# First group of a fused attention + MoE kernel: the weight round moves from the start of a step to the end of the step before, and its last call follows the others

## Chip, cores and metric

The kernel runs on one core of one Trainium2 chip. The metric is device time in microseconds (us) of one launch. Engines are named as in the profile: PE (TensorE matmuls), PEld (TensorE weight loads), DVE (VectorE), ACT (ScalarE), POOL (GpSimd), SP (SyncE; here it only issues DMAs).

## What is computed

Local attention with block summaries, then a feed-forward layer with the Mish activation, all in fp32. Cut from the reference:

```python
B, H, S, D = 4, 8, 768, 64;  block, window = 32, 16
k_sum = k.reshape(B, H, nb, block, D).max(axis=3)       # key maxima per block of 32
v_sum = v.reshape(B, H, nb, block, D).mean(axis=3)      # value means per block of 32
scores = concat(where(|i - j| < 16, scale * q @ k^T, -1e9), scale * q @ k_sum^T + log(32))
x = softmax(scores) @ concat(v, v_sum)                  # -> (3072 tokens, 512)
h = x @ w_in                                            # 512 -> 2048
out = (h * tanh(softplus(h))) @ w_out                   # 2048 -> 512
```

The weights come as 64-bit words (fp64 bits) that the kernel turns into fp32 itself.

## The kernel before

**Units and groups.** Attention works in units (c, hp): 256 queries c and a pair of heads hp; 48 units. Feed-forward works in 6 groups g of 512 tokens, 16 steps fc each (128 of the 2048 hidden columns). Units 0 to 7 are done ahead of the loop; the loop `for i in range(len(steps) + 2)` then does in step i the feed-forward step (g, fc) = divmod(i, 16) and, at the steps in the table `at` (0, 4, 8, 12 in the first group), the scores of two more units, whose values are formed four steps later.

**Order.** The program is under a manual schedule: each engine runs its instructions in the order in which the code emits them, waiting in place for what is not ready. So the order of the calls in a step is the order on every engine and on SP's queue.

**fp32 by splitting.** Each fp32 matmul is three passes: high part times high, high times low, low times high. `ff_in` (L406) gives `ph`, 12 matmuls; `ff_act` (L413) gives `a` (Mish, ACT); `ff_split` gives the high part `ah` (L422, ACT in the first group, DVE later) and the low part `al` (L424, DVE); `ff_out` (L434) adds `w_out`'s part into `po`, 12 matmuls, two steps later.

**Weights, first group only.** 16 pieces, each two steps of `w_in` (w0_k) or `w_out` (w1_k), taken in the order w0_0, w0_2, w1_0, w0_4, w1_2, w0_6, w1_4, w0_8, w1_6, w0_10, w1_8, w0_12, w1_10, w0_14, w1_12, w1_14. A piece passes five calls:

- `load_weight`: two DMAs from SP (L124) into one of two staging buffers. SP waits until `begin_weight` has read the piece that lay there;
- `begin_weight`: `f` on ACT (L136) and `x` on DVE (L138, L140);
- `join_weight`: `f` clamped, shifted and joined with `x` on DVE (L148, L150);
- `upper_weight`: the high part `w_hi` on ACT (L158), which needs the joined `f`;
- `lower_weight`: the low part `w_lo` on DVE (L165), which needs `w_hi`.

I call the first four of them with `lower_weight` a *round*. Each call takes the next piece in its own queue, so a round works on up to five different pieces.

**Attention work that shares the engines.** For a batch (b) and head pair: `ks` is loaded (L201) and its maxima `km` taken on DVE (L244); `vsum` is loaded (L205) into the same buffer (there is one), and its sums `vq` (L264, L265) go out by a DMA `vm` (L266). So the chain is ks, km, vsum, vq, then the next ks. POOL copies `km` into the unit's keys `qk` (L275), and the scores `sc` (L311, PE) of a unit need that copy: first 16 matmuls for the first unit of a pair, then 16 for the second. DVE takes the row maxima `pr`, `nm` (L333), ACT the exponentials (L337), DVE the reciprocals `rs` (L347, L348), POOL the product `pr` (L351). PE transposes (`pt_ps`, L359), ACT copies to `pt` (L361), PE forms `x_ps` (L391), ACT and DVE split it into `xh` (L393) and `xl` (L394).

**A step of the first group before the change**, in the order of the calls: upper, join, begin, load; `rs` and POOL's product (steps 1, 5, 9, 13); `ff_in`, `ff_act`, `ah`; `x_ps` and `xh` (steps 4, 8, 12); scores, maxima and exponentials (steps 0, 4, 8, 12); `lower_weight`; `xl`; `al`; then `vq` or `km` and the DMAs of the attention; `ff_out` of two steps ago; transposes and the `pt` copies (steps 3, 7, 11, 14).

Of the kernel before, what the change touches and what calls it, by code (L numbers as in the profile page):

```python
# [52 lines left out]
def _as_f32(bits):  # L53
    import struct
    return struct.unpack("<f", struct.pack("<I", bits))[0]
# [3 lines left out]
def fused_kernel(ctx: ExitStack, tc: tile.TileContext, q0, qk, kt, v0, vw, vs, w_in, w_out, out):  # L59
# [46 lines left out]
    def home(j, part, dtype, name):  # L106

        if j == NW:
            t = stage.tile([P, WB, WP], I64, tag="stage", name=name).bitcast(dtype)
            return t.rearrange("p k f -> p (k f)")[:, :WB * WP]  # L110
        pool = const if j < EARLY else late[0]
        return pool.tile([P, WB * WP], dtype, tag=f"w{part}_{j}", name=name, bufs=1)
# [6 lines left out]
    def load_weight():  # L119
        if weights:  # L120
            w, fc = weights.pop(0)
            t = stage.tile([P, WB, WP], I64, tag="stage", name=f"w{w}_{fc}")
            for k in range(WB):
                nc.sync.dma_start(t[:, k, :], (w_in, w_out)[w][fc + k])  # L124
            loaded.append((w, fc, t))

    def begin_weight():
        if loaded:
            w, fc, t = loaded.pop(0)
            j = order[w, fc]  # L130
            flat = t.rearrange("p k f -> p (k f)")
            high = flat.bitcast(U32).rearrange("p (f two) -> p f two", two=2)[:, :, 1]
            quarter = flat.bitcast(U16).rearrange("p (f four) -> p f four", four=4)
            x = home(j, 0, U32, f"x{w}_{fc}")
            f = home(j + 1, 1, F32, f"f{w}_{fc}")
            nc.scalar.activation(f, high.bitcast(F32), AF.Copy, scale=2.0 ** -OFFSET)  # L136
            half = x.bitcast(U16).rearrange("p (f two) -> p f two", two=2)
            nc.vector.tensor_scalar(out=half[:, :, 0], in0=quarter[:, :, 1], scalar1=13, scalar2=None,  # L138
                                    op0=ALU.logical_shift_right)
            nc.vector.tensor_scalar(out=half[:, :, 1], in0=quarter[:, :, 3], scalar1=SIGN, scalar2=None,  # L140
                                    op0=ALU.bitwise_and)
            begun.append((w, fc, f, x))

    def join_weight():
        if begun:
            w, fc, f, x = begun.pop(0)
            u = f.bitcast(U32)
            nc.vector.tensor_scalar(out=f, in0=f, scalar1=-_as_f32(F32_MAX), scalar2=_as_f32(F32_MAX),  # L148
                                    op0=ALU.max, op1=ALU.min)
            nc.vector.scalar_tensor_tensor(out=u, in0=u, scalar=3, in1=x,  # L150
                                           op0=ALU.logical_shift_left, op1=ALU.bitwise_or)
            joined.append((w, fc, f))

    def upper_weight():
        if joined:
            w, fc, f = joined.pop(0)
            split[w, fc, 0] = home(order[w, fc], 0, F32R, f"w{w}_{fc}_hi")
            nc.scalar.copy(split[w, fc, 0], f)  # L158
            raised.append((w, fc, f))

    def lower_weight():
        if raised:
            w, fc, f = raised.pop(0)
            split[w, fc, 1] = home(order[w, fc], 1, F32R, f"w{w}_{fc}_lo")
            nc.vector.tensor_sub(split[w, fc, 1], f, split[w, fc, 0].bitcast(F32))  # L165
# [117 lines left out]
    def att_summarize_values(c, hp):  # L283
        b, th = divmod(c, CPB)
        if th == 0:
            value_summary(b, hp)
# [56 lines left out]
    def att_normalize(group):  # L343
        n = len(group) * NQ
        u = units[group[0]]
        rs = small.tile([P, 2 * NQ], F32, tag="rs", name=f"rs{group[0][0]}_{group[0][1]}")[:, :n]
        nc.vector.tensor_scalar_add(rs, u["sm"][:, :n], 1e-9)  # L347
        nc.vector.reciprocal(rs, rs)  # L348
        if u.get("squares"):
            nc.gpsimd.memset(u["wide"][:, :, KA:], 0.0)  # L350
        nc.gpsimd.tensor_mul(u["pr"], u["pr"], rs.unsqueeze(2).broadcast_to([P, n, KA]))  # L351
# [11 lines left out]
    def att_transpose_blocks(group, half):  # L363

        u = units[group[0]]
        if half == 0:
            u["tr"] = att.tile([P, 2 * NQ, P], F32, tag="pt", name=f"pt{group[0][0]}_{group[0][1]}", bufs=1)
            for k, unit in enumerate(group):
                units[unit]["pt"] = u["tr"][:KA, k * NQ:(k + 1) * NQ]
        for a in range(2 * half, 2 * half + 2):  # L370
            for b in range(P // SQ):
                nc.vector.transpose(u["tr"][b * SQ:(b + 1) * SQ, :, a * SQ:(a + 1) * SQ],  # L372
                                    u["wide"][a * SQ:(a + 1) * SQ, :, b * SQ:(b + 1) * SQ])
# [26 lines left out]
    def ff_in(g, fc):  # L400
        xh, xl = xs[g]
        ph = ps_w.tile([P, TG], F32, tag="w", name=f"ph{g}_{fc}")
        wh, wl = (weight(0, part, fc) for part in range(2))
        for cc in range(NCC):
            for n, (w, x) in enumerate(((wh, xh), (wh, xl), (wl, xh))):
                nc.tensor.matmul(ph, w[:, cc * P:(cc + 1) * P], x[:, cc, :],  # L406
                                 start=(cc == 0 and n == 0), stop=(cc == NCC - 1 and n == 2))
        st[g, fc] = ph

    def ff_act(g, fc):  # L410

        a = ff.tile([P, TG], F32, tag="t", name=f"a{g}_{fc}", bufs=2)
        nc.scalar.activation(a, st[g, fc], AF.Mish)  # L413
        st[g, fc] = a

    def ff_split(g, fc):

        a = st[g, fc]
        ah = ff.tile([P, TG], F32R, tag="ah", name=f"ah{g}_{fc}")
        al = ff.tile([P, TG], F32R, tag="al", name=f"al{g}_{fc}")  # L420

        (nc.scalar.copy if g == 0 else nc.vector.tensor_copy)(ah, a)  # L422
        st[g, fc] = ah, al
        return lambda: nc.vector.tensor_sub(al, a, ah.bitcast(F32))  # L424
# [86 lines left out]
    values = dict(zip(turns[1:] + [turns[-1] + 4], (at[i] for i in turns)))  # L511
    turned = {i + (3 if i < NFC - 4 else 2): group for i, group in at.items() if i < NFC - 1}
    following = dict(zip(turns, (at[i] for i in turns[1:])))
    for i in range(len(steps) + 2):
        upper_weight()
        join_weight()
        begin_weight()
        load_weight()
        if i - 1 in at and i < NFC:
            att_normalize(at[i - 1])  # L520
        if i < len(steps):
            ff_in(*steps[i])
            ff_act(*steps[i])
            if i < NFC:
                split_rest = ff_split(*steps[i])
        group = values.get(i)
        lower = att_values(group) if group else None
        if lower and i >= NFC:
            lower()
        if i in at:  # L530
            att_scores(at[i], i >= NFC - 1)
        lower_weight()
        if i < NFC:
            if lower:
                lower()
            split_rest()
        if i - 1 in at and i >= NFC:
            att_normalize(at[i - 1])
        if i - 3 in at and i - 3 >= NFC - 1:
            att_transpose_blocks(at[i - 3], 1)  # L540
        if NFC <= i < len(steps):
            ff_split(*steps[i])()
        if i - 2 in at and i - 2 >= NFC - 1:
            att_transpose_blocks(at[i - 2], 0)
        if i - 3 in following:
            n, m = following[i - 3]
            att_summarize_values(*m)
            after = todo.index(m) + 1
            if after < len(todo) and todo[after][0] % CPB == 0:
                load_key_source(todo[after][0] // CPB, todo[after][1])  # L550
        if i in following:
            n, m = following[i]
            att_summarize_keys(*n)
            for unit in (n, m):
                att_load_keys(*unit)
        if i - 1 in following:
            n, m = following[i - 1]
            att_summarize_values(*n)
            if m[0] % CPB == 0:
                load_key_source(m[0] // CPB, m[1])  # L560
        if i - 2 in following:
            n, m = following[i - 2]
            att_summarize_keys(*m)
            for unit in (n, m):
                att_block_keys(*unit)
        if group:
            for unit in at.get(i, ()):
                att_load_values(*unit)
        if i >= 2:
            ff_out(*steps[i - 2])  # L570
        if i in turned:
            att_transpose(turned[i])
# [44 lines left out]
```

## Time and profile before

| | us |
|---|---|
| median of 3 runs | 633.23 (633.0 to 634.34) |
| the profiled execution | 633.05 |
| its span, first to last instruction | 630.9 |
| PE busy | 604.1 (96%) |
| DVE busy | 385.8 (61%) |
| ACT busy | 258.8 (41%) |
| POOL busy | 78.7 (12%) |

A row of the timeline reads: start in us from the span's start, length in us (of the whole row, where it stands for several instructions, x2), engine, line of the kernel, operation, names out<-in, shapes, and in square brackets the idle time of the engine just before it with what ended it. In the view by windows each row is a stretch: its length, then busy us and number of instructions of PE, PEld, DVE, ACT, POOL, then the TensorE clock granted (1.00 is full), the DMA engines' busy share and GB/s. Consecutive instructions of an engine overlap a little, so what an instruction costs its engine is the distance from its start to the start of the next.

The first matmul of the first group's feed-forward starts at 45.0 us, and its steps 0 to 12 take until about 128 us.

### The profile page before, as it was taken

To read this page: it belongs to the slowest core of one execution; us is meant where nothing else is said; L and a number is where in the kernel's file an instruction comes from. 1 tells how busy PE (TensorE), PEld (TensorE's weight loads), DVE (VectorE), ACT (ScalarE), POOL (GpSimd) and SP (SyncE) were. 2 spreads that over 40 slices of the span, in tenths; PEclk is the share of its full clock that TensorE was granted. 3 is DMA by queue.
4 is the path that set the end of the run, shared out by engine and by line. 5 is a ranking of instruction groups with operands and counts; after the bars stand their busy time and mean duration, and the time that the engine had idled before them with its cause. 6 is when DMAs were issued, how large, how long until landed. Compare 5 with 4: busy or idle time off the path is not lost.

```text
span 630.9 us, 10795 instructions
## 1 busy us (share of the span) xinstructions
PE 604.1 (96%) x4096; PEld 495.1 (78%) x4096; DVE 385.8 (61%) x1032; ACT 258.8 (41%) x630; POOL 78.7 (12%) x119
## 2 busy tenths in 40 slices
PE   5859999799999999999999999999999999999997
PEld 4747887588888888788888888888888888888886
DVE  4678999982855667855656758756647636222221
ACT  3759867675334244245144244153253251111111
POOL 4441020221011011011011010110110110000000
PEclk9979999999999999999999999999999999999999
DMA  8957587733223043533033241532232010100001
GB/s 273 319 191 249 215 271 238 220 115 97 92 72 122 2 146 122 169 98 97 0 98 96 92 147 55 169 99 88 75 97 82 16 33 0 68 0 1 0 1 66
DMA packets 31779, 69.26 MB, mean 110 GB/s; under 512 B 4720, under 2 KB 11120, under 8 KB 31728
## 3 DMA queue, kind: packets, MB, share of 16 engines
q1 hardware_dynamic: 31728, 68.58, 34.2%
q8 instruction: 32, 0.52, 0.4%
q14 instruction: 19, 0.16, 0.1%
HBM read 60.16 MB, written 6.29 MB: 105 GB/s over the span
## 4 chain that ended last, share of the span: by engine, by line
PE 78%; DMA 7%; DVE 7%; ACT 3%; issue 2%; SPq 1%; POOL 0%; DVEq 0%; ACTq 0%; POOLq 0%
PE po L434 37%; PE ph L406 35%; DMA vw<-vw 3%; PE x_ps L391 3%; PE sc L311 3%; DMA w<-w_out 2%; DMA w<-w_in 1%; DVE w_lo L165 1%; DVE al L424 1%; DVE x L138 1%; ACT f L136 1%; ACT pr L337 1%; DVE x L140 1%; DVE f L148 1%; DMA ks<-kt 1%
## 5 line engine op out<-in xcount | busy, mean ns | idle before, releaser
L413 ACT ACTIVATE a<-ph 128x512 f32<-128x512 f32 x96 | 57.2, 596 | 284.1 <-PE ph L406 230.6
L434 PE MATMUL po<-w_hi,ah 128*128 128x512 f32 x384 | 152.0, 396 | 0.7 <-ACT ah L422 0.5
L434 PE MATMUL po<-w_hi,al 128*128 128x512 f32 x384 | 149.9, 390 | 1.4 <-DVE al L424 1.4
L406 PE MATMUL ph<-xh,w_hi 128*128 128x512 f32 x384 | 150.7, 393 | 0.0
L406 PE MATMUL ph<-xl,w_hi 128*128 128x512 f32 x384 | 150.2, 391 | 0.0
L406 PE MATMUL ph<-xh,w_lo 128*128 128x512 f32 x384 | 150.0, 391 | 0.0
L434 PE MATMUL po<-w_lo,ah 128*128 128x512 f32 x384 | 149.6, 390 | 0.0
L422 DVE CAST ah<-a 128x512 fp32r<-128x512 f32 x80 | 34.6, 433 | 144.1 <-ACT a L413 143.6
L372 DVE STREAM_TRANSPOSE pt<-pr 32x256 f32<-32x256 f32 x256 | 111.5, 436 | 3.6
L434 PEld LDWEIGHTS po<-w_hi,ah 128*128 128x128 f32 x384 | 72.1, 188 | 19.0 <-issue 3.0
L434 PEld LDWEIGHTS po<-w_hi,al 128*128 128x128 f32 x384 | 72.1, 188 | 16.7 <-DVE al L424 2.5
L406 PEld LDWEIGHTS ph<-xh,w_hi 128*128 128x128 f32 x384 | 72.6, 189 | 15.2 <-issue 0.2
L406 PEld LDWEIGHTS ph<-xh,w_lo 128*128 128x128 f32 x384 | 72.5, 189 | 15.2
L406 PEld LDWEIGHTS ph<-xl,w_hi 128*128 128x128 f32 x384 | 72.5, 189 | 14.9
L434 PEld LDWEIGHTS po<-w_lo,ah 128*128 128x128 f32 x384 | 72.1, 188 | 15.2
L337 ACT ACTIVATE pr<-pr,nm 128x120 f32<-128x120 f32 x192 | 73.2, 383 | 14.8 <-DVE nm L333 14.6
L351 POOL TENSOR_TENSOR pr<-pr,rs 128x960 f32<-128x960 f32 (+1 forms) x28 | 47.4, 1692 | 221.8 <-DVE rs L348 131.8
L424 DVE TENSOR_TENSOR al<-a,ah 128x512 fp32r<-128x512 f32 x96 | 69.7, 726 | 5.9 <-ACT ah L422 3.1
L391 PEld LDWEIGHTS x_ps<-pt,vw 120*64 120x64 f32 x768 | 25.7, 141 | 21.3 <-issue 8.6
L391 PE MATMUL x_ps<-pt,vw 120*64 120x64 f32 x768 | 29.4, 229 | 12.7 <-ACT pt L361 5.4
L394 DVE TENSOR_TENSOR xl<-x_ps,xh 128x512 fp32r<-128x512 f32 (+1 forms) x28 | 17.2, 614 | 34.9 <-ACT xh L393 34.5
L337 ACT ACTIVATION_READ_ACCUMULATOR pr<-pr,nm 128x1 f32 x192 | 35.9, 187 | 0.0
(59 smaller groups left out, 451.4 us busy)
## 6 DMA issues: line engine op xcount, KB each, us to landing
qk<-qk SPq DMA_DIRECT2D x40, 496.0 KB, 4.1
vw<-vw SPq DMA_DIRECT2D x48, 192.0 KB, 5.1
w<-w_in SPq DMA_DIRECT2D x16, 512.0 KB, 5.2
w<-w_out SPq DMA_DIRECT2D x16, 512.0 KB, 5.2
ks<-kt SPq DMA_DIRECT2D x16, 384.0 KB, 4.4
out<-o SPq DMA_DIRECT2D x24, 256.0 KB, 2.3
vsum<-vs SPq DMA_DIRECT2D x12, 384.0 KB, 3.4
vw<-vm SPq DMA_DIRECT2D x40, 48.0 KB
```

The source lines that it names most:

```text
L136: nc.scalar.activation(f, high.bitcast(F32), AF.Copy, scale=2.0 ** -OFFSET)
L311: nc.tensor.matmul(ps[h][row, at0:at0 + KA], u["qk"][r, s, h * QT:(h + 1) * QT], u["qk"][r, s, P:], start=True, stop=True)
L337: nc.scalar.activation(pr[:, j, :], pr[:, j, :], AF.Exp, scale=-1.0, bias=nm[:, j:j + 1], accum_out=sm[:, j:j + 1])
L351: nc.gpsimd.tensor_mul(u["pr"], u["pr"], rs.unsqueeze(2).broadcast_to([P, n, KA]))
L372: nc.vector.transpose(u["tr"][b * SQ:(b + 1) * SQ, :, a * SQ:(a + 1) * SQ], u["wide"][a * SQ:(a + 1) * SQ, :, b * SQ:(b + 1) * SQ])
L391: nc.tensor.matmul(x, u["v"][:, s, d], pt, start=True, stop=True)
L394: return lambda: nc.vector.tensor_sub(xl, x, xh.bitcast(F32))
L406: nc.tensor.matmul(ph, w[:, cc * P:(cc + 1) * P], x[:, cc, :], start=(cc == 0 and n == 0), stop=(cc == NCC - 1 and n == 2))
L413: nc.scalar.activation(a, st[g, fc], AF.Mish)
L422: (nc.scalar.copy if g == 0 else nc.vector.tensor_copy)(ah, a)
L424: return lambda: nc.vector.tensor_sub(al, a, ah.bitcast(F32))
L434: nc.tensor.matmul(po[g][t], a[:, tok], w, start=(fc == 0 and n == 0), stop=(fc == NFC - 1 and n == 2))
```

## The change

The round is taken from the head of a step and put behind `al` of the step before, with `lower_weight` as its last call; ahead of the loop one round without `upper_weight` is done. The same instructions run, as many as before, on the same engines; the order changes on DVE, on ACT, on SP and so what PE waits for.

```diff
+    lower_weight()
+    join_weight()
+    begin_weight()
+    load_weight()
     for i in range(len(steps) + 2):
-        upper_weight()
-        join_weight()
-        begin_weight()
-        load_weight()
         if i - 1 in at and i < NFC:
             att_normalize(at[i - 1])
...
         if i in at:
             att_scores(at[i], i >= NFC - 1)
-        lower_weight()
         if i < NFC:
             if lower:
                 lower()
             split_rest()
+        upper_weight()
+        join_weight()
+        begin_weight()
+        load_weight()
+        lower_weight()
         if i - 1 in at and i >= NFC:
             att_normalize(at[i - 1])
```

How the rows of an engine stand, at the places on which the prediction rests. A row is line, operation, out<-in, shape; the last number of a name is the tile's own (it differs between the two kernels), the ones ahead of it are group or piece and step (`al0_9`: step 9 of group 0) or batch and head pair (`vq1_2`).

DVE from `al` of step 9 to the key maxima `km1_3`, before:

```order
L424 TENSOR_TENSOR al0_9_1366<-a0_9_1363,ah0_9_1365 128x512
L264 TENSOR_REDUCE vq1_2_1372<-vsum1_2_1310 96x32
L265 TENSOR_SCALAR vq1_2_1372<-vq1_2_1372 96x32
L148 TENSOR_SCALAR f0_14_1339<-f0_14_1339 128x1024
L150 SCALAR_TENSOR_TENSOR f0_14_1339<-f0_14_1339,x0_14_1338 128x1024
L138 TENSOR_SCALAR x1_12_1394<-w1_12_1228 128x1024
L140 TENSOR_SCALAR x1_12_1394<-w1_12_1228 128x1024
L165 TENSOR_TENSOR w1_10_lo_1417<-f1_10_1224,w1_10_hi_1390 128x1024
L424 TENSOR_TENSOR al0_10_1415<-a0_10_1412,ah0_10_1414 128x512
L244 TENSOR_REDUCE km1_3_1420<-ks1_3_1376 128x24
```

and after (the five rows of the round that now follow `al0_9` directly are L148 and L150 on f0_14, L138 and L140 on x1_12, and the first row here):

```order
L165 TENSOR_TENSOR w1_10_lo_1380<-f1_10_1192,w1_10_hi_1371 128x1024
L264 TENSOR_REDUCE vq1_2_1383<-vsum1_2_1324 96x32
L265 TENSOR_SCALAR vq1_2_1383<-vq1_2_1383 96x32
L424 TENSOR_TENSOR al0_10_1417<-a0_10_1414,ah0_10_1416 128x512
L148 TENSOR_SCALAR f1_12_1376<-f1_12_1376 128x1024
L150 SCALAR_TENSOR_TENSOR f1_12_1376<-f1_12_1376,x1_12_1375 128x1024
L138 TENSOR_SCALAR x1_14_1424<-w1_14_1317 128x1024
L140 TENSOR_SCALAR x1_14_1424<-w1_14_1317 128x1024
L165 TENSOR_TENSOR w0_14_lo_1429<-f0_14_1313,w0_14_hi_1420 128x1024
L244 TENSOR_REDUCE km1_3_1431<-ks1_3_1387 128x24
L424 TENSOR_TENSOR al0_11_1465<-a0_11_1462,ah0_11_1464 128x512
```

`vq1_2` went from ahead of the round to behind it, and so did `km1_3`; between `vq` and `km` DVE has one `al` and one round either way.

ACT at the turn from step 3 to step 4, before:

```order
L422 CAST ah0_3_897<-a0_3_895 128x512
L361 COPY pt2_0_917<-pt_ps2_0_918 120x512
L361 COPY pt2_0_917<-pt_ps2_1_924 120x512
L158 CAST w1_4_hi_930<-f1_4_824 128x1024
L136 ACTIVATE f1_6_935<-w1_6_828 128x1024
L413 ACTIVATE a0_4_955<-ph0_4_942 128x512
```

and after:

```order
L422 CAST ah0_3_899<-a0_3_897 128x512
L158 CAST w1_4_hi_903<-f1_4_824 128x1024
L136 ACTIVATE f1_6_908<-w1_6_828 128x1024
L361 COPY pt2_0_931<-pt_ps2_0_932 120x512
L361 COPY pt2_0_931<-pt_ps2_1_938 120x512
L413 ACTIVATE a0_4_957<-ph0_4_944 128x512
```

The two `pt` copies, for which `x_ps` of step 4 waits, went behind `w_hi` and `f` of the round; the same at steps 7/8 and 11/12 (there with no `f`).

SP's queue at the same place, from `vsum1_2` to `ks1_3`, before:

```order
L124 DMA w1_12_1228<-w_out 128x512 x2
L205 DMA vsum1_2_1310<-vs 96x1024
L270 DMA qk3_2_1312<-qk 128x992
L270 DMA qk3_3_1314<-qk 128x992
L224 DMA vw3_0_1316<-vw 96x512
L290 DMA vw3_0_1316<-vm1_0_1084 24x4x128
L224 DMA vw3_1_1319<-vw 96x512
L290 DMA vw3_1_1319<-vm1_1_1187 24x4x128
L124 DMA w1_14_1343<-w_out 128x512 x2
L266 DMA vm1_2_1371<-vq1_2_1372 24x4x32
L201 DMA ks1_3_1376<-kt 128x768
```

and after:

```order
L124 DMA w1_14_1317<-w_out 128x512 x2
L205 DMA vsum1_2_1324<-vs 96x1024
L270 DMA qk3_2_1326<-qk 128x992
L270 DMA qk3_3_1328<-qk 128x992
L224 DMA vw3_0_1330<-vw 96x512
L290 DMA vw3_0_1330<-vm1_0_1098 24x4x128
L224 DMA vw3_1_1333<-vw 96x512
L290 DMA vw3_1_1333<-vm1_1_1201 24x4x128
L266 DMA vm1_2_1382<-vq1_2_1383 24x4x32
L201 DMA ks1_3_1387<-kt 128x768
```

The load of the last piece, w1_14, went ahead of the attention's loads; the others keep their order.

## Prediction

> **What bounds the kernel now.** First the page: which engine is full.
>
> ```profile
> PE 604.1 (96%) x4096; PEld 495.1 (78%) x4096; DVE 385.8 (61%) x1032; ACT 258.8 (41%) x630; POOL 78.7 (12%) x119
> ```
>
> PE is, over the whole span. The view by windows then tells the stages apart: the last steps of the change's reach, and all that follows.
>
> ```profile
> 115.00:128.00 13.00, 9.05 (x98) 7.23 (x98) 11.74 (x15) 6.49 (x10) 1.95 (x3) 1.00 0.63 182
> 128.00:631.00 503.00, 498.86 (x3092) 410.17 (x3090) 280.30 (x788) 168.49 (x427) 47.29 (x65) 1.00 0.24 75
> ```
>
> From 128 us on PE is busy 498.86 of 503.00 us, so it takes up no lateness and gives none back: what the first group gains or loses by then moves the end one for one. In 115 to 128 PE is busy only 9.05 of 13.00, DVE 11.74. So third, PE's timeline, for where it waits or nearly does.
>
> ```profile
> 69.70 1.15 PE L391 MATMUL x_ps<-pt,vw 120*64 120x64 f32 x32
> ...
> 96.27 1.18 PE L391 MATMUL x_ps<-pt,vw 120*64 120x64 f32 x32 [1.54 <-ACT pt L361]
> ...
> 116.38 0.50 PE L434 MATMUL po<-w_hi,al 128*128 128x512 f32 x1 [1.18 <-DVE al L424]
> ...
> 122.41 0.39 PE L406 MATMUL ph<-xh,w_lo 128*128 128x512 f32 x1
> 125.57 1.17 PE L391 MATMUL x_ps<-pt,vw 120*64 120x64 f32 x32 [2.77 <-ACT pt L361]
> 126.67 1.05 PE L311 MATMUL sc<-qk 64*64 64x120 f32 x32
> 127.65 0.50 PE L434 MATMUL po<-w_hi,ah 128*128 128x512 f32 x1
> ```
>
> The waits are for the `pt` copies at steps 8 and 12 (1.54, 2.77) and for `al` of step 9 (1.18); at step 4 `x_ps` runs at 69.70 without one. The last wait counts most: whatever is late or early before it is late or early into it, and `po` at 127.65 is where the lossless part begins. So I ask what starts this `po` after the change, and walk there.
>
> Fourth, DVE's timeline from step 9 to step 11, the engine on whose order most is moved.
>
> ```profile
> 112.83 0.20 DVE L348 RECIPROCAL rs<-rs 128x8 f32<-128x8 f32 x1
> 112.95 1.17 DVE L165 TENSOR_TENSOR w_lo<-f,w_hi 128x1024 fp32r<-128x1024 f32 x1
> 114.04 2.28 DVE L424 TENSOR_TENSOR al<-a,ah 128x512 fp32r<-128x512 f32 x1
> 116.25 1.21 DVE L264 TENSOR_REDUCE vq<-vsum 96x32 f32<-96x1024 f32 x1
> 117.49 0.18 DVE L265 TENSOR_SCALAR vq<-vq 96x32 f32<-96x32 f32 x1
> 117.58 0.68 DVE L148 TENSOR_SCALAR f<-f 128x1024 f32<-128x1024 f32 x1
> 118.30 1.23 DVE L150 SCALAR_TENSOR_TENSOR f<-f,x 128x1024 uint32<-128x1024 uint32 x1
> ...
> 121.86 0.68 DVE L424 TENSOR_TENSOR al<-a,ah 128x512 fp32r<-128x512 f32 x1
> 123.69 0.95 DVE L244 TENSOR_REDUCE km<-ks 128x24 f32<-128x768 f32 x1 [1.16 <-DMA ks<-kt]
> 124.56 0.68 DVE L148 TENSOR_SCALAR f<-f 128x1024 f32<-128x1024 f32 x1
> 125.28 1.23 DVE L150 SCALAR_TENSOR_TENSOR f<-f,x 128x1024 uint32<-128x1024 uint32 x1
> ```
>
> No idle time but the 1.16 ahead of `km`: DVE is what paces these steps. A round on it takes 121.86 - 117.58 = 4.28 us. And POOL beside it:
>
> ```profile
> 113.21 2.57 POOL L351 TENSOR_TENSOR pr<-pr,rs 128x960 f32<-128x960 f32 x1 [17.09 <-DVE rs L348]
> 115.72 0.72 POOL L275 COPY qk<-km 128x96 f32<-128x96 f32 x1
> 124.86 0.51 POOL L275 COPY qk<-km 128x96 f32<-128x96 f32 x1 [8.42 <-DVE km L244]
> ```
>
> `al` took 2.28 at 114.04 against 0.68 at 121.86: it ended 0.54 after POOL's product (113.21 + 2.57 = 115.78), so DVE stood 1.60 us while POOL worked.
>
> **The change part by part.** No instruction is added or dropped. Up to step 3 nothing is won: ACT's order is the old one until the first `pt` copies, and rounds and `al` alternate on DVE as before (`w_lo` and `al` only change what precedes them). I cost this at nothing; its cover is that ACT's `ah` of step 1 releases PE in both kernels. If that failed, the DVE chain below would shift with it.
>
> *Step 4: the `pt` copies behind `w_hi` and `f`.*
>
> ```profile
> 68.77 1.06 ACT L361 COPY pt<-pt_ps 120x512 f32<-120x512 f32 x2
> 70.17 1.05 ACT L158 CAST w_hi<-f 128x1024 fp32r<-128x1024 f32 x1 [0.33 <-DVE f L150]
> 71.67 1.16 ACT L136 ACTIVATE f<-w 128x1024 f32<-128x1024 f32 x1 [0.45 <-DMA w<-w_out]
> 72.72 0.60 ACT L413 ACTIVATE a<-ph 128x512 f32<-128x512 f32 x1
> ```
>
> `w_hi` waited for DVE and `f` for a weight DMA, neither of which the change brings forward here. So the copies start where `a` did, 72.72, the first of the two (some 0.58 to its end; the row's 1.06 holds both, a little overlapped) is done at 73.30, and `x_ps` starts at about 73.33 and not at 69.70: PE is 3.63 us late, a new wait.
>
> *Steps 5 and 9: `al` ahead of POOL's product.* Now `rs` stands directly before `al`, and POOL starts 113.21 - 112.83 = 0.38 after the reciprocal, when `al` (0.12 after it) runs. `al` comes 1.6 earlier, so the wait of 1.18 at 116.38 goes; but the next on DVE, L148, finds POOL at work. The trace has no L148 behind POOL's product. From below: it runs on, and DVE gains 1.60 at each of the two steps; from above: it stands as `al` did, gain 0. I take 0, since the two do hold each other up in the other order: the POOL copy at 124.86 took 0.51, ended at 125.37 just behind L148's end (124.56 + 0.68 = 125.24), and the median copy takes this:
>
> ```profile
> L275 POOL COPY qk<-km x40: 262/267/1140, 40.0 to 492.1; 128x96 f32<-128x96 f32 x40
> ```
>
> [...]
>
> *Step 8.* The round's L150 comes ahead of `km` now:
>
> ```profile
> 87.81 1.20 DVE L264 TENSOR_REDUCE vq<-vsum 96x32 f32<-96x1024 f32 x1
> ...
> 93.41 0.69 DVE L424 TENSOR_TENSOR al<-a,ah 128x512 fp32r<-128x512 f32 x1
> 94.44 0.95 DVE L244 TENSOR_REDUCE km<-ks 128x24 f32<-128x768 f32 x1 [0.33 <-DMA ks<-kt]
> ```
>
> `al` of step 6 at 93.41 stays (the same work precedes it); then 0.60 + 0.72 + 1.23 to the end of L150 at 95.96, `w_hi` 1.05, `f` 1.15, the first copy 0.58: `x_ps` at about 98.65 and not at 96.27, +2.4. PE, 3.63 late less the old wait of 1.54, would come at 98.36, so it waits 0.3. From there to the end of `ph` in step 12 (122.41 + 0.39 = 122.80) everything follows 2.4 later less the 1.18 that is gone: 124.0.
>
> *Step 12, `x_ps`.* `al` of step 10 stays at 121.86; then L148 and L150 directly (`km` behind them): 121.86 + 0.60 + 0.72 + 1.23 = 124.41; `w_hi` 1.05 and the first copy 0.58: 126.05, against 125.57. The last piece's load, ahead in SP's queue now, has landed by then; it was what held ACT before. +0.5, and PE, ready at 124.0, waits 2.0.
>
> *Step 12, scores.* Their second half needs POOL's copy of `km1_3`, at the end of the chain vq, DMA out, `ks` load, `km`, copy. `vq` moves behind the round: 114.04 + 0.60 + 1.60 + 4.28 = 120.52 and not 116.25. From a `vq` to its `km` went 123.69 - 116.25 = 7.44 here and 94.44 - 87.81 = 6.63 four steps earlier. I take 6.63: the longer one shared the DMA engines with the last weight piece, which is out of the way now. `km` at 127.15; from its start to the end of the copy 125.37 - 123.69 = 1.68: 128.83. Half of the scores' 0.98 (126.67 to 127.65) is still to do: `po` at 129.35 and not 127.65. **+1.7 us.** Ends: DVE alone, with `ks` there in time, is ready for `km` at 120.52 + 1.33 (117.58 - 116.25) + 0.60 + 4.28 = 126.73, +1.3; with 7.44, +2.5.
>
> The qk and ks loads also move behind weight loads on SP; their readers come 3.6 us later at step 4 or are the chain just counted. Queued behind the late scores on PE is `po`, and then all the rest, without a wait to absorb it.
>
> Against the profiled execution: 633.05 + 1.7 = 634.75. It lies 0.18 below the median, 633.23, so I say **634.9**.
>
> **The rivals.** *Faster: L148 is not held.* DVE would gain 1.60 at step 5 and again at step 9. `vq` at 117.3, `km` at 123.95, copy done at 125.63; `x_ps` when PE comes, 124.0; `po` at 126.15: -1.5, 631.7. For it: no row shows L148 standing. Against it: the copy held by L148. It decides from a gain on DVE of 1.7 + 1.27 = 3.0 us on, so it takes both steps; with one, 633.3, it is no change. *No change: the chain to the scores is shorter.* With `ks` in time (+1.3) or one collision gone (+0.1) it ends between 633.3 and 634.5. For it: DVE's 1.16 and 0.33 ahead of the two `km` show that a faster load would be used at once; against it: both rows have it waiting. *Slower by more:* 7.44 again, or `al` and `w_lo` waiting for an ACT that PE, 3.6 late, holds up: 635.7 and above. The PE lateness as such is no rival: at step 12 it has 2.0 us of cover.
>
> **How the numbers follow.** A measurement of this kernel can tell about 0.2%, 1.27 us, from no change. Forecast, 634.5 to 635.6: 0.48. More: 0.12. No change: 0.24. Faster: 0.16. So slower 0.60, same 0.24, faster 0.16. The likeliest case's own range is 634.5 to 635.8; to leave out no more than 2 in 10 I go from 632.0, near the faster case, to 636.4.
>
> **What would show it.** Right: a PE wait of about 3.6 ahead of `x_ps` at 73.3 with ACT's `pt` named; no wait for `al` of step 9; L148 of 2.2 us or more behind POOL's product; a wait inside the scores of step 12 for POOL's copy of `km`, near 128.8, and `km` with an idle gap for `ks`. Wrong: L148 of 0.7 there and `vq` of step 9 before 119; or scores of step 12 in one piece.

## The result, and the profile after

| | before | after |
|---|---|---|
| median, us (12 runs each) | 634.37 (632.57 to 636.48) | 638.5 (636.12 to 642.06) |
| ratio of the runs | | 1.0064, 95% interval 1.0043 to 1.0084 |
| the profiled execution (its span) | 633.05 (630.9) | 637.34 (635.2) |

The change makes the kernel 4.1 us slower; 1.7 were forecast. The page's line of engines, and the view by windows of the stretches shown of before:

```profile
PE 607.9 (96%) x4096; PEld 498.6 (78%) x4096; DVE 386.6 (61%) x1032; ACT 259.2 (41%) x630; POOL 75.6 (12%) x119
```

```profile
115.00:128.00 13.00, 11.65 (x56) 9.39 (x54) 12.86 (x18) 8.74 (x12) 2.31 (x2) 1.00 0.86 258
128.00:631.00 503.00, 501.18 (x3156) 412.32 (x3156) 281.28 (x789) 169.50 (x429) 47.89 (x66) 1.00 0.24 74
```

From 128 us on PE is as full as before. So the loss is there by the `po` of step 12, and PE's timeline of after shows it whole:

```profile
73.90 1.98 PE L391 MATMUL x_ps<-pt,vw 120*64 120x64 f32 x32 [4.09 <-ACT pt L361]
75.81 1.88 PE L311 MATMUL sc<-qk 64*64 64x120 f32 x32
...
101.61 1.17 PE L391 MATMUL x_ps<-pt,vw 120*64 120x64 f32 x32 [0.45 <-ACT pt L361]
...
128.35 1.17 PE L391 MATMUL x_ps<-pt,vw 120*64 120x64 f32 x32 [1.70 <-ACT pt L361]
129.45 0.64 PE L311 MATMUL sc<-qk 64*64 64x120 f32 x16
131.37 0.64 PE L311 MATMUL sc<-qk 64*64 64x120 f32 x16 [1.28 <-POOL qk L275]
131.94 0.50 PE L434 MATMUL po<-w_hi,ah 128*128 128x512 f32 x1
```

`po` begins at 131.94 and not at 127.65: 4.29, the difference of the spans (4.3). It waits where the prediction said, inside the scores for POOL's copy, but 2.6 us later than its 129.35. Two things stand out that were not forecast: after the wait of 4.09 at step 4, `x_ps` takes 1.98 and the scores 1.88, where the same two rows take 1.17 and 1.05 at step 8; and, on DVE's timeline of after, the wait in the third row:

```profile
86.71 2.28 DVE L148 TENSOR_SCALAR f<-f 128x1024 f32<-128x1024 f32 x1
92.59 1.21 DVE L264 TENSOR_REDUCE vq<-vsum 96x32 f32<-96x1024 f32 x1
...
100.94 0.95 DVE L244 TENSOR_REDUCE km<-ks 128x24 f32<-128x768 f32 x1 [2.05 <-DMA ks<-kt]
...
122.85 1.21 DVE L264 TENSOR_REDUCE vq<-vsum 96x32 f32<-96x1024 f32 x1
...
129.05 0.94 DVE L244 TENSOR_REDUCE km<-ks 128x24 f32<-128x768 f32 x1
```

These are L148 beside POOL's product (2.28, as in the forecast's case), `vq1_0` and `km1_1`, `vq1_2` and `km1_3`. `km1_3` waits for nothing: the gap for `ks` that the prediction expected there is not in the trace. Last, POOL's timeline of after, the product and the copy of `km1_3`:

```profile
86.40 2.05 POOL L351 TENSOR_TENSOR pr<-pr,rs 128x960 f32<-128x960 f32 x1 [18.60 <-DVE rs L348]
...
130.20 1.11 POOL L275 COPY qk<-km 128x96 f32<-128x96 f32 x1 [6.61 <-PE sc L311]
```

The copy took 1.11 and not 0.51: `al` and the next L148 stand beside it on DVE (129.91 to 131.19). It needs `km`, which ended at 129.99; the profile names the scores because their first half ended 0.1 us later (130.09). In before the copy ran ahead of these scores (124.86 against 126.67), so it does not need them.

### The profile page after: what moved, and what is told of

Same layout as the page of the kernel before. It is cut to its first block, busy times and chain, and to the rows that moved or that the text cites. A ratio compares the mean times of both kernels' runs of the same rounds, so it can differ in the third digit from the quotient of the medians.

```text
span 635.2 us, 10797 instructions
## 1 busy us (share of the span) xinstructions
PE 607.9 (96%) x4096; PEld 498.6 (78%) x4096; DVE 386.6 (61%) x1032; ACT 259.2 (41%) x630; POOL 75.6 (12%) x119
## 4 chain that ended last, share of the span: by engine, by line
PE 79%; DMA 8%; DVE 6%; ACT 4%; issue 2%; SPq 1%; POOL 0%; POOLq 0%; ACTq 0%; DVEq 0%
PE po L434 37%; PE ph L406 35%; PE x_ps L391 4%; DMA vw<-vw 3%; PE sc L311 3%; DMA w<-w_out 2%; DMA qk<-qk 1%; ACT f L136 1%; DMA w<-w_in 1%; DMA ks<-kt 1%; DVE f L148 1%; DVE x L138 1%; ACT w_hi L158 1%; DVE pr L333 1%; DVE al L424 1%
## 5 line engine op out<-in xcount | busy, mean ns | idle before, releaser
L424 DVE TENSOR_TENSOR al<-a,ah 128x512 fp32r<-128x512 f32 x96 | 67.1, 699 | 6.9 <-ACT ah L422 4.1
L351 POOL TENSOR_TENSOR pr<-pr,rs 128x960 f32<-128x960 f32 (+1 forms) x28 | 44.5, 1591 | 216.6 <-DVE rs L348 147.5
L391 PE MATMUL x_ps<-pt,vw 120*64 120x64 f32 x768 | 30.7, 235 | 14.3 <-ACT pt L361 8.0
L333 DVE CUSTOM_DVE_ANT_0 pr<-sc,base 128x120 f32<-128x120 f32 x128 | 31.5, 278 | 7.7 <-PE sc L311 6.9
```

The lines of the kernel that those rows point to most:

```text
L333: nc.vector.tensor_tensor_reduce(out=pr[:, j, :], in0=ps[h][:, at0:at0 + KA], in1=m, scale=-SCALE, scalar=-NEG, op0=ALU.add, op1=ALU.min, ...
L391: nc.tensor.matmul(x, u["v"][:, s, d], pt, start=True, stop=True)
```

## The experiments

The start-up differs by execution: the scores of step 0 begin between 48.8 and 51.8 us, whatever the kernel. So beside the times the table has the distance from there to `po` of step 12 in the one profile of each run. (The run of a profile can stand off its median: in e10, e11 and e14 by 2.1, 1.5 and 3.0 us above it, in e8 and f3 by 2.0 and 1.6 below it. Their distances may be off likewise.) Ratios are to the kernel before on the same chip; 0.001 is 0.63 us.

| run | median | ratio, 95% interval | scores of step 0 to `po` of step 12 |
|---|---|---|---|
| before | 634 to 635 | 1 | 77.93 |
| after | 638.5 | 1.0064 (1.0043 to 1.0084) | 82.56 |
| f5, after again | 639.09 | 1.0065 (1.0050 to 1.0081) | 82.80 |
| e1, round behind the sums | 636.76 | 1.0045 (1.0025 to 1.0065) | 80.85 |
| e2, `pt` first | 635.75 | 1.0032 (1.0011 to 1.0053) | 81.06 |
| e4, before with `lower_weight` up | 634.47 | 1.0003 (0.9984 to 1.0021) | 78.14 |
| e5, weight load behind | 638.08 | 1.0058 (1.0037 to 1.0079) | 82.24 |
| e7, qk behind ks | 640.38 | 1.0089 (1.0066 to 1.0112) | 82.59 |
| e10, first km ahead | 640.76 | 1.0099 (1.0073 to 1.0125) | 83.71 |
| e11, first qk behind ks | 639.51 | 1.0070 (1.0051 to 1.0089) | 84.75 |
| e13, `pt` first and first qk | 638.47 | 1.0058 (1.0040 to 1.0076) | 82.21 |
| e14, product later | 637.14 | 1.0045 (1.0028 to 1.0061) | 83.90 |
| e12, clock kept | 636.18 | 1.0022 (1.0008 to 1.0035) | 79.18 |
| g2, e12 again | 635.79 | 1.0023 (1.0006 to 1.0040) | 79.00 |
| g1, two extra matmuls | 639.17 | 1.0072 (1.0040 to 1.0103) | 81.19 |
| f1, e1 with the clock kept | 636.78 | 1.0028 (1.0012 to 1.0044) | 79.41 |
| f3, before with late `pt` | 634.42 | 1.0000 (0.9986 to 1.0015) | 78.35 |
| f4, f3 with the clock kept | 634.72 | 0.9999 (0.9984 to 1.0014) | 77.13 |
| e9, before, qk behind ks | 634.05 | 0.9988 (0.9970 to 1.0006) | 76.99 |
| e8, e4 and qk behind ks | 632.78 | 0.9972 (0.9956 to 0.9989) | 76.04 |

### Each half of the order undone: e1, e2, e4

e1 puts the round behind the attention's calls, e2 the transposes ahead of the round, e4 takes of the change only the place of `lower_weight`:

```diff
e1 (after)
         split_rest()
-        upper_weight()
-        join_weight()
-        begin_weight()
-        load_weight()
-        lower_weight()
...
+        upper_weight()
+        join_weight()
+        begin_weight()
+        load_weight()
+        lower_weight()
         if i >= 2:
             ff_out(*steps[i - 2])
e2 (after)
+        if i in turned:
+            att_transpose(turned[i])
         upper_weight()
e4 (before)
         load_weight()
+        lower_weight()
...
-        lower_weight()
```

> The kernel after with one edit: the round (with lower_weight at its end) stands behind the attention's sums, maxima and their DMAs, just ahead of ff_out. So vq of step 9 stands ahead of the round on DVE again, and km of step 11 too, and the weight load stands behind the attention's loads on SP; the pt copies on ACT stay behind w_hi and f, as after. Theory A (the end is set at step 12 by the chain vq, ks, km, POOL's copy, second half of the scores): the 4.3 us that po of step 12 lost come back, about 634 (633 to 635.3), although the wait ahead of x_ps at step 4 stays (3.5 to 4.5 us) and PE's clock falls after it. Theory B (PE's lateness at step 4 is the cause and is handed on): the time stays at 637 or above.

> The kernel after with one edit: at steps 3, 7 and 11 the transposes and the pt copies stand ahead of the round, so on ACT the two copies come before w_hi and f; the order of DVE and SP stays that of after. Theory A (chain vq, ks, km, POOL's copy): x_ps of step 4 starts near 70 without its 4 us of wait, PE's clock stays full there, and yet the time falls by only the 0.5 us by which the slow scores held DVE: -0.3 to -1.2 against after, 637.3 to 638.2; the second half of the scores of step 12 still waits for POOL's copy. Theory B (PE's lateness at step 4): -3.6 to -4.3, 634.2 to 635.

> The kernel before with one edit: lower_weight is called at the head of the step right behind load_weight, not after the scores. So rs of steps 5 and 9 stands directly ahead of al on DVE (as after), POOL's product runs beside al's end and what follows it, vq and not L148; the pt copies, km, vq and SP's order stay as before. Theory A: where the instruction behind al is vq (a reduction) and it runs on beside POOL, DVE gains up to 1.6 us at steps 5 and 9, and the wait for al at step 9 (1.18) goes: 632 to 633.3, 1 to 2 us under before. Rival: w_lo waits on DVE for ACT's w_hi at the head of the step, or vq is held by POOL as al was: within 0.6 us of before, or slower by up to 1.

Neither theory had e1 or e2. Each edit takes back a part of the 4.1 us: by the ratios 1.2 (e1) and 2.0 (e2), by the medians 1.7 and 2.8; the intervals overlap those of after, e1's widely. Each leaves one limit at step 12 standing. PE's timeline of e1, where `x_ps` waits for the late `pt`:

```profile
130.34 1.17 PE L391 MATMUL x_ps<-pt,vw 120*64 120x64 f32 x32 [2.54 <-ACT pt L361]
131.45 1.05 PE L311 MATMUL sc<-qk 64*64 64x120 f32 x32
```

and of e2, where the second half of the scores waits for POOL's copy:

```profile
101.18 1.08 PE L311 MATMUL sc<-qk 64*64 64x120 f32 x16 [4.58 <-POOL qk L275]
...
129.91 0.64 PE L311 MATMUL sc<-qk 64*64 64x120 f32 x16 [1.28 <-POOL qk L275]
```

Behind the wait of 4.58 at step 8 the clock halved in e2 too: its sixteen matmuls took 1.08, those of the second row 0.64. So e2 is free of the half clock of step 4 alone. e1 has `km` ahead of the round again, so L150, `w_hi` and the copies come behind it; the prediction's +0.5 for `x_ps` of step 12 held only with `km` out of the way. In e1 `km1_1` and `km1_3` also waited for `ks`, 2.72 and 1.80 us, so it is not a clean removal of the late chain. e4, with both halves as before, is no different from before. Its DVE timeline shows a gain made and given back:

```profile
87.31 0.65 DVE L424 TENSOR_TENSOR al<-a,ah 128x512 fp32r<-128x512 f32 x1
87.88 1.21 DVE L264 TENSOR_REDUCE vq<-vsum 96x32 f32<-96x1024 f32 x1
...
97.01 0.95 DVE L244 TENSOR_REDUCE km<-ks 128x24 f32<-128x768 f32 x1 [2.48 <-DMA ks<-kt]
```

POOL's product ran at 87.57 for 2.04, beside `vq`; `vq` kept its 1.21 and `al` its 0.65, so the 1.60 were DVE's, and the wait for `ks` (2.48 against 0.33 of before) took them.

### The loads ahead of ks: e5, e10, e7, e11, e13

e5 issues the weight load of steps 0 to 7 behind the attention's loads; e10 puts `km1_0` and `km1_2` with their loads ahead of the round; e7 moves the qk loads behind the ks load, e11 those of step 4 alone, e13 is e11 with the transposes of e2:

```diff
e5 (after)
-        load_weight()
+        if i >= 8:
+            load_weight()
...
+        if i < 8:
+            load_weight()
e10 (after)
+        if i in following:
+            n, m = following[i]
+            att_summarize_keys(*n)
+            for unit in (n, m):
+                att_load_keys(*unit)
         upper_weight()
e7 (after; e11: only at i == 4 and 5)
             att_summarize_keys(*n)
-            for unit in (n, m):
-                att_load_keys(*unit)
...
                 load_key_source(m[0] // CPB, m[1])
+            for unit in (n, m):
+                att_load_keys(*unit)
```

> The kernel after with one edit: in steps 0 to 7 the weight load is issued behind the attention's loads of the step, not ahead of them (SP's order alone; from step 8 on as after). Theory C (of the 2.6 us that the prediction missed, some 2 are the wait of km1_1 at step 7 for its ks, and that comes from SP standing at 78.3 to 84.0 on a weight load with the attention's loads queued behind it): the wait of 2.05 us ahead of km1_1 shrinks to under 0.5, the DMA engines are not empty at 82 to 84, and the time falls by 1.5 to 2.2 us against after, 636.2 to 637. Rival D (the DMA engines are simply full, whatever the order): the wait stays at 1.5 to 2.5 and the time within 0.6 us of after, 638 to 639.

> The kernel after with one edit: of the attention's sums and maxima, only the key maxima of steps 4 and 8 (km1_0, km1_2) go ahead of the round again, with the loads of vsum and qk that follow them; vq and the other km stay behind it. Theory A (km1_0 behind the round frees the one buffer of ks and vsum 5 us later, SP holds vsum, qk and vw back, the DMA engines stand empty at 82 to 84 and are full at 88 to 102, and so km1_1 waits 2.05 us for its ks): vsum is issued near 81.5 and not at 86.2, the hole at 82 to 84 closes, the wait ahead of km1_1 falls under 0.7, and po of step 12 starts 1.5 to 2.5 earlier against the scores of step 0: -1.3 to -2.3 against after, 636.2 to 637.2. Rival B (ks comes when the bytes in front of it are through, whatever km1_0 does): the wait stays at 1.5 to 2.7 and the time within 0.7 of after, 637.8 to 639.2.

> The kernel after with one edit: the two qk loads of a batch's turn are issued one step later, behind the next ks load, not in front of it (SP's order alone). Theory B (ks waits behind bytes): with the two qk loads behind it, ks of km1_1 lands about 2 to 3 us earlier, the wait of 2.05 ahead of km1_1 goes, and so does most of the 2.4 us that f waits for its weights there: -1.3 to -2.2 against after, 636.2 to 637.2. Rival C (the wait is set by SP's standing and by when vq is done, not by bytes): the wait stays over 1.2 and the time within 0.7 of after.

> The kernel after with one edit: only the two qk loads of step 4 go one step later, behind the ks load of step 5; those of steps 8 and later stay (in e7, which moved all, km1_1 found its ks in time, but the scores of step 12 then waited for the late qk and po ran at half clock). Theory B (the wait for ks, 1.7 us more than the prediction allowed, is carried by DVE to step 12): km1_1 starts without a wait, al of step 7 comes 2 to 3 us earlier, po of step 12 1.5 to 2.5 earlier against the scores of step 0, no half clock there: -1.3 to -2.4 against after, 636.1 to 637.2. Rival (the gain on DVE meets another wait before step 12): within 0.7 of after.

> The kernel after with two edits: the transposes and pt copies ahead of the round (as in e2) and the two qk loads of step 4 behind the ks load of step 5 (as in e11). What is left of the change is then the later vq and km alone, without the late x_ps and without the long wait for ks. Theory A: the chain vq, ks, km, POOL's copy then costs what the prediction gave it, po of step 12 1.3 to 2.3 later than before against the scores of step 0; e2 less 1 to 1.5, so 634.2 to 635.3. Rival (the chain costs what e2 showed, whatever ks does): 635.4 to 636.3.

(`km1_1` and `km1_3` are issued in steps 6 and 10; the first texts count them a step later.) Not one of the five made the kernel faster, and each shows the wait in a new place. In e5 `vsum` went out at 86.57, behind `km1_0` as before the edit, and DVE waited for weights in place of `ks`:

```profile
99.30 0.77 DVE L138 TENSOR_SCALAR x<-w 128x1024 uint16<-128x1024 uint16 x1 [2.11 <-DMA w<-w_in]
```

In e10 `km1_0`, now early, waited for its own `ks`:

```profile
84.83 0.95 DVE L244 TENSOR_REDUCE km<-ks 128x24 f32<-128x768 f32 x1 [2.73 <-DMA ks<-kt]
```

In e7 `km1_1` found its `ks` (no wait), so bytes do stand in front of it; but the copies of step 12 waited for the late qk, and PE, which had stood 1.54, 0.64 and 1.89 us with only `x_ps` and scores between, began the lossless part at half clock. PE's timeline and the view by windows of e7:

```profile
131.71 1.08 PE L311 MATMUL sc<-qk 64*64 64x120 f32 x16 [1.89 <-POOL qk L275]
132.72 0.79 PE L434 MATMUL po<-w_hi,ah 128*128 128x512 f32 x1
```

```profile
132.00:134.00 2.00, 2.00 (x19) 1.50 (x14) 1.90 (x2) 0.00 (x0) 0.00 (x0) 0.50 0.01 4
```

There the clock has no cover: the 12 matmuls of that `po` took 5.5 us in place of 3.0. In e10 and e11 the lossless part began at half clock as well: from the start of `po` of step 12 to the next `ph` it is 4.85 and 3.85 us, against 2.85 in before and after, which their distances in the table do not hold. In e11 (and e13, 2.75) the next `vq` waited:

```profile
108.97 1.22 DVE L264 TENSOR_REDUCE vq<-vsum 96x32 f32<-96x1024 f32 x1 [2.92 <-DMA vsum<-vs]
```

So no run showed that the wait for `ks`, taken away alone, is worth its 2 us: in these orders another load is late in its place, and in e7, e10 and e11 the half clock of step 12 comes on top, so the theory was not tested by itself.

### The clock at step 4: e12, g1, g2, f5, f1, f3, f4

e12 gives PE ten matmuls ahead of `x_ps` of step 4, in its own bank, which `x_ps` then overwrites; g1 gives it two:

```diff
         ps = att_psum(c, f"x_ps{c}_{hp0}")
+        for _ in range(10 if (c, hp0) == todo[CG * HP] else 0):
+            nc.tensor.matmul(ps, weight(0, 0, 0)[:, :P], xs[0][0][:, 0, :], start=True, stop=True)
```

> The kernel after with ten extra matmuls of 128x512 into the bank of x_ps of step 4, ahead of x_ps (which overwrites them): PE works 2.4 of the 4.1 us in which it waits there. Theory (the half clock behind that wait makes x_ps and the scores 1.7 us slower and DVE 0.4 to 0.5 later): x_ps starts when it did, takes 1.15 and not 1.98, the scores 1.05 and not 1.88, the granted clock stays 1.00 from 74 to 78, al of step 4 comes 0.4 to 0.5 earlier: -0.3 to -0.8 against after. Rival (PE's clock at step 4 is covered): within 0.2 of after in the time, with al of step 4 unmoved.

> e12 with two extra matmuls ahead of x_ps of step 4 in place of ten: PE still stands about 3.6 us. Theory K (the gain of e12 goes with the clock kept at full): the clock halves at 74 to 78, km1_1 waits 1.5 to 2.5 us for ks, the time is that of after, 637.8 to 639.3. Rival (it comes from something else that the extra matmuls bring): wait under 0.7 and 635.5 to 636.8.

> e12 unchanged, for a second profile. If its short wait for ks belongs to the kernel: km1_1 waits under 0.7 us again and the time is 635.7 to 636.8. If it was one execution: a wait of 1.5 to 2.5 in this profile, with the time still under that of after by the 0.5 us of the slow scores alone, 637 to 638.5.

> The kernel after, unchanged, beside the others on the same chip, with a profile of another execution. If the wait of km1_1 for ks (2.05 us) belongs to the kernel, it is 1.5 to 2.5 again; if it varies with the execution, it may be anything from 0 to 3. The time 637.5 to 639.5.

This is the largest single piece, and more than my theory for e12 had (0.3 to 0.8): e12 and g2 stand 2.3 and 2.7 us under after by the medians. By the ratios the change, with the clock kept, costs 0.22% or 1.4 us (0.4 to 2.5 between the ends of both intervals). g1, which has the edit but stands 3.57 us and halves its clock, costs what after does by its median and ratio; its times scatter widely (635.5 to 641.2), and its distance, 81.19, lies between those of after and e12. The views by windows of after and of e12, at step 4 and over the transfers before `km1_1`:

```profile
74.00:78.00 4.00, 4.00 (x65) 3.58 (x66) 3.61 (x5) 3.33 (x5) 0.00 (x0) 0.50 0.54 203
86.00:98.00 12.00, 12.00 (x57) 9.96 (x57) 11.87 (x15) 7.37 (x9) 2.31 (x2) 1.00 1.00 304
```

```profile
74.00:78.00 4.00, 3.58 (x70) 3.09 (x71) 3.97 (x6) 3.74 (x6) 0.00 (x0) 1.00 0.61 227
86.00:98.00 12.00, 12.00 (x59) 10.01 (x58) 11.86 (x16) 7.40 (x9) 2.90 (x2) 1.00 1.03 350
```

and DVE's timeline of e12, `vq1_0` and `km1_1`:

```profile
92.61 1.21 DVE L264 TENSOR_REDUCE vq<-vsum 96x32 f32<-96x1024 f32 x1
...
99.04 0.95 DVE L244 TENSOR_REDUCE km<-ks 128x24 f32<-128x768 f32 x1
```

The five profiles of this order side by side:

| | clock 74 to 78 | wait of `km1_1` for `ks` | `vq1_0` to `km1_1` | GB/s, 86 to 98 |
|---|---|---|---|---|
| after | 0.50 | 2.05 | 8.35 | 304 |
| f5 | 0.50 | 2.41 | 8.79 | 299 |
| g1 | 0.57 | 2.42 | 8.78 | 321 |
| e12 | 1.00 | 0.1 | 6.43 | 350 |
| g2 | 1.00 | under 0.1 | 6.22 | 344 |

So the wait belongs to the kernel, and in this order it goes with the clock of step 4 (e2, with the full clock there and the same order on DVE and SP, lies between, with 0.89). In other orders it does not: `km1_1` waited 2.48 in e4 and 2.43 in f1, both at full clock at step 4. The scores at half clock hold DVE directly for 0.5 us only (`al` of step 4 at 80.08, 79.57 before). A part of the way from there to `ks` stands in SP's queue. SP's timelines of after and of e12, the DMA `vm` of `vq1_0` and the `ks` load of `km1_1`:

```profile
94.03 0.81 SPq L266 DMA_DIRECT2D vm<-vq  x1
95.24 0.34 SPq L201 DMA_DIRECT2D ks<-kt  x1
```

```profile
94.06 0.80 SPq L266 DMA_DIRECT2D vm<-vq  x1
94.91 0.51 SPq L201 DMA_DIRECT2D ks<-kt  x1
```

Ahead of these two, SP stood 1.1 us in after, 2.5 in f5 and 1.9 in g1, by the profile for the `qk` loads; in e12, g2 and e2 not at all. So the `ks` load went out 2.65, 3.71 and 3.24 us after the start of `vq1_0`, and 2.30, 2.29 and 2.30 in the other three. SP stood so in e1, e4 and f1 too (1.0 to 1.3), where `km1_1` waited 2.4 to 2.7. Why the `qk` loads land later behind the half clock is not shown: the DMA engines are as busy in all five profiles (share 1.00 to 1.03) and move less. That the half clock alone does not do it, f3 shows. It gives the kernel before the late `pt` copies of step 3, and nothing else; f4 is f3 with the ten matmuls, f1 is e1 with them:

```diff
f3 (before)
         load_weight()
+        if i == NFC // 4:
+            att_transpose(turned[i - 1])
...
-        if i in turned:
+        if i in turned and i != NFC // 4 - 1:
             att_transpose(turned[i])
```

> The kernel before with one edit: the transposes and pt copies of step 3 stand behind the round at the head of step 4, on ACT behind w_hi and f; all else as before. So x_ps of step 4 waits 3.4 to 4.1 us and PE's clock halves, and nothing else of the change is there. Theory H: 1.5 to 2.5 over before. Rival (as the prediction had it: PE's waits of 1.54, 1.18 and 2.77 at steps 8, 9 and 12 cover the lateness): within 0.6 of before.

> f3 with the ten extra matmuls ahead of x_ps of step 4: as late as in f3, but at full clock. Theory H: within 0.6 of before. If the lateness itself costs, and not the clock: as f3, 1.5 to 2.5 over before, if f3 is slower at all.

> e1 (the round behind the attention's sums, maxima and loads; pt copies behind w_hi and f) with the ten extra matmuls ahead of x_ps of step 4, as in e12. Theory H (the half clock at step 4 costs about 2 us, the late x_ps of step 12 little): 634.4 to 635.4, 1.4 to 2.4 under e1. Rival (e1 loses its 2.3 us at step 12, where x_ps waits for the late pt copies): 636.2 to 637.2, as e1.

PE's timeline of f3:

```profile
72.65 1.97 PE L391 MATMUL x_ps<-pt,vw 120*64 120x64 f32 x32 [3.46 <-ACT pt L361]
74.56 1.88 PE L311 MATMUL sc<-qk 64*64 64x120 f32 x32
...
100.42 1.15 PE L391 MATMUL x_ps<-pt,vw 120*64 120x64 f32 x32
```

The wait and the half clock are there, and the time is that of before (1.0000; f4 0.9999): in before's order PE's lateness is covered, as the prediction had it, and `vq1_0` to `km1_1` is 6.21. My theory H, that the clock costs 2 us by itself, is wrong for before's order. f1 does not decide: its median is e1's, its ratio 1.1 us lower with overlapping intervals, and its clock halved at step 8 instead (scores 1.88 behind a wait of 2.53).

### POOL's product elsewhere: e14

```diff
e14 (after)
-        if i - 1 in at and i < NFC:
-            att_normalize(at[i - 1])
...
         lower_weight()
-        if i - 1 in at and i >= NFC:
+        if i - 1 in at:
             att_normalize(at[i - 1])
```

> The kernel after with one edit: in the first group the reciprocals and POOL's product go behind the round, so that the product does not run beside L148 of steps 5 and 9. Theory (the product holds L148): L148 takes 0.69 and not 2.29 at both places, and what then stands beside the product is vq, which runs on (in e4 it took 1.20 there), and the start of al: DVE gains 0.8 to 1.6 at each step; at step 5 part of it goes into the wait for ks: po of step 12 1 to 2.4 earlier, 636.1 to 637.5. Rival (POOL's product takes its 1.6 us from DVE wherever it stands): L148 0.69, but vq or al of the next step 2.2 or more, and the time within 0.7 of after.

L148 of steps 5 and 9 takes 0.69, and at step 2, where the moved product now meets it, 2.28. DVE's and POOL's timelines of e14:

```profile
69.58 2.28 DVE L148 TENSOR_SCALAR f<-f 128x1024 f32<-128x1024 f32 x1
...
89.32 0.69 DVE L148 TENSOR_SCALAR f<-f 128x1024 f32<-128x1024 f32 x1
```

```profile
69.25 2.06 POOL L351 TENSOR_TENSOR pr<-pr,rs 128x960 f32<-128x960 f32 x1 [26.96 <-DVE rs L348]
```

The product holds L148 in each order in which they met (after, e14). What that is worth is not measured: the transposes of step 3 now wait 3.97 us for the product, the clock halves there (0.53 granted from 70 to 74 us), and the ratio is 1.2 us under that of after with overlapping intervals.

### A faster version: e8, e9

e8 is e4 with the qk loads of e7, e9 is before with them.

> The kernel before with lower_weight at the head of the step (as in the run e4) and the two qk loads one step later, behind the ks load. In e4 DVE gained 1.6 us at step 5 and gave it back waiting 2.5 us for ks. Theory B: ks lands earlier, the waits of 2.5 and 2.1 ahead of km1_1 and km1_3 fall under 1 each, DVE keeps its gain, x_ps of steps 8 and 12 comes 1 to 2.5 earlier: -1 to -2.4 against before, 632.1 to 633.5. Rival: the pt copies then wait on ACT for f's weights instead (the same DMA engines): within 0.7 of before.

> The kernel before with the two qk loads one step later, behind the ks load, and nothing else. Theory B: the waits of 0.33 and 1.16 us ahead of km1_1 and km1_3 go; the pt copies at step 12 that waited for the last weights come a little earlier: -0.3 to -1.2 against before. Rival: nothing on the path to x_ps of step 12 is moved by it: within 0.4 of before.

e8 beats both kernels: 0.9972 (0.9956 to 0.9989), 1.8 us under before. DVE keeps what `lower_weight` up gave it at step 5; `km1_1` in e8 starts without a wait, and `po` of step 12 is there at 124.84:

```profile
92.63 0.95 DVE L244 TENSOR_REDUCE km<-ks 128x24 f32<-128x768 f32 x1
```

```profile
122.52 1.17 PE L391 MATMUL x_ps<-pt,vw 120*64 120x64 f32 x32 [0.41 <-ACT pt L361]
...
124.84 0.50 PE L434 MATMUL po<-w_hi,ah 128*128 128x512 f32 x1
```

Either part alone is not told from before (e4 1.0003, e9 0.9988): the first needs `ks` early to be worth anything.

## Why the prediction was right in kind and wrong in size

- *Sign and place:* right. `po` of step 12 waits inside the scores for POOL's copy, the wait for `al` of step 9 is gone, `x_ps` of step 4 waits for `pt`. One sign failed: `km1_3` has no gap for `ks`. The wait at step 4 is 4.09 against 3.63; the weights of `f` landed 0.57 later than in the profile of before.
- *L148 held:* right, 2.28 twice (0.68 to 0.76 elsewhere), ending 0.54 and 0.55 after the product, as `al` did in before (0.54). So L148 is held behind the product in after, and in e14 (2.28 against 0.69), while `vq`, a reduction, runs on beside it in e4 (1.21). The faster rival fell with that.
- *Step 4, the step that failed:* "The PE lateness as such is no rival: at step 12 it has 2.0 us of cover". The lateness is covered (f3), but a wait of 4 us is more than lateness. I priced it at full clock, with DVE's maxima unmoved and `vq1_0` to `km1_1` as before. They measured +0.51 on DVE, and 8.35 in place of 6.63. Together 2.2: `vq` of step 9 is at 122.85 and not at 120.52, 2.3 late. With the clock kept (e12, g2) the change costs 1.4 by the ratios, and the forecast's 1.7 lies within their intervals.
- *The chain at step 12:* `vq` to `km` took 129.05 - 122.85 = 6.20 against the 6.63 taken (0.43 back). That is DVE's own work, the 1.33 + 0.60 + 4.28 = 6.21 of the prediction's lower end; the load was in time. The copy took 1.11 against 0.51 (0.6 more): I had left out that `al` and L148 now follow `km1_3` directly. So 2.3 - 0.4 + 0.6 = 2.5 of the 2.6 that were missing. The 0.6 does not follow from the order alone: with the same rows behind `km1_3` the copy took 1.11 in after, f5 and e2, and 0.51 in e12, g2 and g1. So 0.6 of the 3.4 between the distances of after and e12 is this copy, and is not shown to be the clock's.
- *The rivals:* "slower by more" named 7.44 at the second chain, and an ACT held up by the late PE. It was the first chain that grew. The second limit at step 12, `x_ps` behind the copies, I had at 126.05; in after it stands at 128.35, 2.3 late like `vq`. Without the wait for POOL's copy `po` could begin at 129.45 + 0.98 = 130.43 (an estimate, with the scores' 0.98 of before), so the chain alone sets only the last 1.5 us. That is why much remains when only one of the two is undone.

Shown is that the wait for `ks` comes with the half clock in this order (three profiles against two), that the clock alone does not make the loss (f3), and that none of the other orders of loads (e5, e7, e10, e11, e13) mended it. SP's stand for the `qk` loads is a part of the way between; from the slow scores to the later `qk` loads it stays open.

## What to carry to other kernels

A new wait ahead of the matrix engine is priced with what may follow it at half clock (in after `x_ps` took 1.98 and the scores 1.88 behind 4.09 us of wait, in place of 1.17 and 1.05), and with who reads those results, not as lateness alone; some matmuls into a bank that will be overwritten are a cheap test of that (in e12 and g2 ten kept the granted clock at 1.00 from 74 to 78 us; two, in g1, left it at 0.57). Where several chains end within 2 us of each other (here `pt`, `km` by POOL, and the bytes in front of `ks`), undoing one shows the next, so the parts of a change are tried in a square (both, either, none). A gain on an engine that then waits for a load is worth nothing until the load is earlier too: e4 and e9 gave nothing that could be told, together they gave 1.8 us.

## What the hardware showed that I had not expected

- The granted clock fell from 1.00 to 0.50 behind waits of 4.09 (after), 3.57 (g1) and 3.46 (f3), but also behind 2.41 (e4: scores of step 8 at 1.88), 2.53 (f1) and 2.65 (e11, step 12), while 2.77 (before, step 12), 2.54 (e1, step 12) and 3.66 (e13, first half of the scores of step 8 at 0.64) left it full. So the length of one wait does not decide it: 2.41 halved it, and 2.54, 2.77 and 3.66 did not. What decides it is not shown. By windows of 0.5 us the granted clock fell at about 72.0 in after, 2.2 us after PE's last matmul (69.42 + 0.39), and at about 99.5 in e4, when `x_ps` (98.80) was already at work.
- Short work did not keep the clock: in e7 three waits of 1.54, 0.64 and 1.89, with `x_ps` and 16 score matmuls between them, halved it (0.50 granted from 132 to 138 us).
- In the order of after, DMA engines that are full all the same (share 1.00 to 1.03 from 86 to 98) moved 299 to 321 GB/s in the three profiles with the half clock at step 4 and 344 to 350 in the two without. The rate does not go with the clock in other orders: at full clock it was 315 in before and e4 and 299 in f4 (shares 0.97 and 0.98).
